# H3 convolution with a bilinear gated unit, forward and backward: forward sums of 2048 elements, a sixth transform by eight residues, early rows in single PSUM banks, filter rows turned whole

## The chip, the cores and the metric

One core of one Trainium2 chip. The metric is the device time of one execution in microseconds: the time before is the median of 3 runs. Engines: PE (TensorE, matrix multiplications and their weight loads), DVE (VectorE), ACT (ScalarE), POOL (GpSimd), SP (SyncE, which issues transfers).

## What is computed

The forward pass, and the gradients of all inputs for a given output gradient, of

```python
xn = layernorm(x)                                  # x = A_q, [2048, 1024]
kv = shift4(k, shift_k) * v                        # causal, four taps, by channel
y  = irfft(rfft(kv padded to 4096) * rfft(ssm_k padded to 4096))[:2048] + kv * ssm_D
g  = silu(((xn @ w_gate) * (xn @ w_up)) @ w_down)  # 1024 -> 3584 -> 1024
out = x + (xn * y) * g
```

for a sequence of 2048 rows and 1024 channels; inputs and outputs are bf16.

## The kernel before

**The matrix part.** The layer norm is made in six chunks of 128-row blocks: blocks (0,1), (1,1), (2,2), (4,4), (8,4), (12,4), written (first, count). DVE takes statistics (L584, L585), ACT a square root (`half_r`, L592), DVE a reciprocal and the normalization (L603). The rows are then turned on PE (as weights, against an identity) into PSUM and copied by ACT to `XNT`: blocks 0 and 1 in halves (L609, L610), 2 to 7 whole (L620, L621), 8 to 15 by `turn_late` (L631 copies, L571 turns). `gu_unit` multiplies them with slabs of `w_gate` and `w_up` (L673, tile `psg`); ACT casts the result (L675, `gut`), DVE forms `h` (tile `hN`, a product of 128x1024; `hN_s` in the first chunks), PE turns it (`turn_pair`, L571, or L724), and it is stored. The last turn of `hN` is made by `flush()`, some steps into the next part, in which h is multiplied with `w_down` (L1032, tile `psbm`, by `bm_first`; 28 steps `fc`, of four matmuls each). The load of the later rows of `w_down` and of `HT` follows the flush on SP. After that comes the backward pass (L1480 to L1642).

**The convolution.** It runs beside the matrix part, slice after slice of 128 channels (`ds` 0 to 7). A generator, `conv_forward`, is advanced by `tick`, which compares the weights that it yields (`F_TOTAL` is their sum, `pe_us` the PE time charged to them) with the progress of the matrix part. Its operations are pinned, so on each engine the order is the order of the program. For each slice there are two forward transforms, of the filter (`hx`) and of `kv`, then a product of spectra and an inverse. A forward transform has a part on PE (`psF`, L234), an eviction by ACT to `SP` (L295) and butterflies on DVE. It takes one of two forms: four residues (`fwd4_half`, 32 matmuls psF of 128x256 per transform) or eight (`fwd8_half` and `fwd8`, 16 matmuls and more of DVE). `EIGHT` lists (slice, kind) in the second form, with kind 0 for `kv` and 1 for the filter; `INV8` lists the slices whose inverse goes by eight. The DVE sums W <- SP are of 128x1024, and `SP` has two buffers, one for each half of the transform.

**The filter rows.** `h_rows(ds)` turns a slice of `ssm_k`: sixteen column blocks of 128, read with a stride of eight elements, each in two halves of 64 rows on two parts of the array (`turn_halves`, L571), into one tile `tr` of the one-buffer pool `ps_tr`; ACT copies it to `hx` (L791).

**PSUM early on.** The early turns take banks of one tile `turns` in `ps_st`, of four banks in a ring (`next_bank`); `keep_busy` writes one of them with dummy matmuls (L534).

What sets the order around the change is the program order for the pinned operations, and for the rest (`issue_after` lines, the layer norm's chunks) a scheduler. The order in which the engines run is fixed when the kernel is built.

Of the kernel before, what the change touches and what calls it, by code (L numbers as in the profile page):

```python
# [19 lines left out]
def build_kernel(  # L20
# [11 lines left out]
    nc = tc.nc  # L32
# [210 lines left out]
    def net(w):  # L243
        w -= 0.95 * pe_us[0]
        pe_us[0] = 0.0
        return w

    def fwd4_half(x, i, wp, psp, first=None):

        pe_us[0] += 1.75  # L250
        SP = wp.tile([P, 2, 2, 512], F32, name="SP", bufs=2)
        for par in range(2):
            ps = psp.tile([P, 2, 2, 256], F32, name="psF")
            cmm(ps[:, 0], T4[par], x, (i, i + 4), first if i == 0 else None, True)
            cmm(ps[:, 1], T4[par], x, (i + 2, i + 6))
            nc.scalar.copy(out=SP[:, :, par], in_=ps[:].rearrange("p s k x -> p s (k x)"))
        return SP

    def fwd4_buf(wp):
        return wp.tile([P, 2, 2, 4, 256], F32, name="W", tag="W")  # L260

    def fwd4_sums(W, SP, i):
        s, q = [SP[:, j].rearrange("p a (k x) -> p (a k) x", k=2) for j in range(2)]
        tt(W[:, 0, i], s, q, ADD)
        tt(W[:, 1, i], s, q, SUB)

# [19 lines left out]

    def fwd8_half(x, i, SP, psp, first=None, held=False):

        pe_us[0] += 0.87
        for j in range(2):  # L290
            r = 2 * i + j
            ps = psp.tile([P, 2, 2, 256], F32, name="psF")
            cmm(ps[:, 0], T4[0], x, (r,), first if r == 0 else None, held)
            cmm(ps[:, 1], T4[0], x, (r + 4,))
            nc.scalar.copy(out=SP[:, :, j], in_=ps[:].rearrange("p s k x -> p s (k x)"))  # L295

    def fwd8(SPs, X, W, C, ahead, late=False):
# [5 lines left out]
        for i in range(2):  # L303
            s, q = [SPs[i][:, j].rearrange("p a (k x) -> p (a k) x", k=2) for j in range(2)]
            tt(W[:, 4 * i:4 * i + 4, :], s, q, ADD)
            tt(W[:, 4 * i + 8:4 * i + 12, :], s, q, SUB)
            yield 2.5
# [213 lines left out]
    ps_gu = pool("ps_gu", 2, space=PSUM)  # L521
    ps_st = pool("ps_st", 1, space=PSUM)
    turns = ps_st.tile([P, 4, 2, 4, P], BF16, name="tr")
    bank = [0]

    def next_bank():
        bank[0] += 1
        return turns[:, bank[0] % 4]

    busy = turns[:, 0].rearrange("p a b x -> p (a b x)").bitcast(F32).rearrange("p (a x) -> p a x", a=4)  # L530

# [45 lines left out]
    def layer_norm(b0, n, x4):  # L577
# [22 lines left out]
        for i in range(n):  # L600
            b = b0 + i
            q, qi = divmod(b, 4)
            last = V.tensor_scalar(x4[:, i, :], x4[:, i, :], mv[:, i, 0:1], RSTD[:, b:b + 1], op0=SUB, op1=MUL)  # L603
            if b < 2:
                for hh in range(2):
                    ps = next_bank()[:, 0]
                    for dc in range(4):
                        d0 = (4 * hh + dc) * P
                        tr_ln[0] = nc.tensor.transpose(ps[:, dc, :], x4[:, i, d0:d0 + P], ident[:])  # L609
                    act_copy[0] = nc.scalar.copy(out=XNT[0][:, 4 * hh:4 * hh + 4, b * P:b * P + P], in_=ps)  # L610
                if b == 0:
                    with tc.issue_after(tr_ln[0].ins):
                        keep_busy(10)
                continue
            if b0 >= 8:
                turn_rows.append((x4[:, i, :], q, qi))
                continue
            ps = next_bank().rearrange("p a b x -> p (a b) x")
            for dc in range(DC):
                tr_ln[0] = nc.tensor.transpose(ps[:, dc, :], x4[:, i, dc * P:(dc + 1) * P], ident[:])  # L620
            act_copy[0] = nc.scalar.copy(out=XNT[q][:, :, qi * P:(qi + 1) * P], in_=ps)  # L621
        c, r0 = divmod(b0, 8)
        return last, root, st(xnn[:, c, r0:r0 + n, :], x4[:, 0:n, :])

    def turn_late():
        ps = turns[:].rearrange("p (h j) i b x -> p h j i (b x)", h=2).rearrange("p h j i (a u) -> p h (j i) a u", u=64)
        for i, (x, q, qi) in enumerate(turn_rows):
            for dc in range(DC):
                tr_ln[0] = turn_halves(lambda hh: ps[:, hh, i, dc], x[:, dc * P:(dc + 1) * P])
        for i, (x, q, qi) in enumerate(turn_rows):  # L630
            act_copy[0] = nc.scalar.copy(out=halves(XNT[q][:, :, qi * P:(qi + 1) * P]), in_=ps[:, :, i])  # L631
        turn_rows.clear()
# [100 lines left out]
    ht_st = [None]  # L733
    EIGHT = ((0, 0), (0, 1), (6, 0), (7, 0), (7, 1))
    INV8 = (2, 4, 5, 6, 7)
# [6 lines left out]
    def conv_forward():  # L742
# [35 lines left out]

        def h_rows(ds):
            if ds == 8:  # L780
                return
            hrow = S_["h", ds]
            hx = S_["hx"] = cf.tile([P, NB, P], BF16, name="hx")
            pe_us[0] += 0.67
            ps = tr_tile()[:].rearrange("p h b x -> p h (b x)").rearrange("p h (b u) -> p h b u", u=64)
            with tc.issue_after(tr_ln[0].ins):
                turn_halves(lambda hh: ps[:, hh, 0], hrow[:, 0, :, 0])
            for b in range(1, 16):
                turn_halves(lambda hh: ps[:, hh, b], hrow[:, b // 8, :, b % 8])
            for c in range(2):  # L790
                nc.scalar.activation(halves(hx[:, 8 * c:8 * c + 8, :]), ps[:, :, 8 * c:8 * c + 8], ACT.Copy, scale=WSC)  # L791
            h_out.append(ds)
            if ds + 1 < 8:
                load_h(ds + 1)

# [30 lines left out]
        def half(ds, x, i, first=None):  # L826
            if (ds, int(first is not None)) not in EIGHT:
                return fwd4_half(x, i, cf, ps_cv, first)
            SP = cf.tile([P, 2, 2, 512], F32, name="SP", bufs=2)
            fwd8_half(x, i, SP, ps_cv, first, True)  # L830
            return SP

        def transform(ds, kind, sp, X, C, ahead, step):
# [10 lines left out]
            W = fwd4_buf(cs)  # L844
            fwd4_sums(W, sp[0], 0)
            step()
# [15 lines left out]
        yield 3.9  # L862
        h_rows(0)
        yield 0.1
        tl = turn_tables(ps_cv)
        sp = [half(0, S_["hx"], i, Dz[:, 0:P]) for i in range(2)]
        for ds in range(8):
# [18 lines left out]
            def behind():  # L886
                calls.append(0)
                if len(calls) % 2 == 0:
                    next(tl, None)
            room = cf.tile([P, 4, 256], F32, name="room", tag="hx")[:] if eight else None  # L890
            yield from transform(ds, int(ds > 0), sph, HX if ds else KX, room, nop1 if eight else lambda c: h_rows(ds + 1) if c == 0 else None,
                                 behind)
            if ds == 0:
                S_["kst"] = st(KFd[0], KX[:])
            if eight:
                h_rows(ds + 1)
            turned(HX, 1, 0, 1)
            yield 1.3
            if ds == 7:
                cf.release()  # L900
                S_["filters"] = False
# [20 lines left out]

    F_TOTAL = 4 * SHIFT_W + 3.0 + 8 * (0.5 + FWD4_W + 1.3 + PROD_W + INV_W) + 10.0 - 0.95 * 8 * (4 * 1.75 + 0.67 + 4 * 0.9)
    F_TOTAL += len(EIGHT) * (FWD8_W - 9.6 + 0.95 * 1.75) - 2.0
# [49 lines left out]
    for p_ in (lnp, lns, tg, bsb):  # L974
        p_.release()
    ps_st.release()
    ps_cv = pool("ps_cv", 2, space=PSUM)
# [70 lines left out]
    pss = [ps_bm.tile([P, D], F32, name="psbm") for i in range(2)]  # L1048
    with tc.issue_after(bm_first(range(4)).ins):
        flush()  # L1050
# [14 lines left out]
    with tc.issue_after(wd_ld.ins):  # L1065
        ht1 = load_ht1()
    fc_ = 4
    while conv_state["filters"]:
# [737 lines left out]
```

## Time and profile before

| | us |
|---|---|
| median of 3 runs (lowest to highest) | 1915.76 (1915.60 to 1915.89) |
| profiled execution, its own time | 1915.97 |
| its span | 1914.2 |
| PE busy (share of span) | 1895.2 (99%) |
| DVE busy | 1550.7 (81%) |
| ACT busy | 637.1 (33%) |
| POOL busy | 334.8 (17%) |
| share of PE in the chain that ended last | 96% |

A line of a timeline reads: start in us, duration of the group, engine, source line and operation, output<-input, array tile and size, count, and in brackets the idle time ahead of it and what released it. A line of the groups reads: busy time of all, mean ns of one, and after the bar the idle time ahead. A line of the waits reads: the engine and what it waited to do, the instruction that released it, the total in us, how many times, the longest. The TensorE clock granted in this execution was 0.999 of full.

### The profile page before, as it was taken

To read this page: it belongs to the slowest core of one execution; us is meant where nothing else is said; L and a number is where in the kernel's file an instruction comes from. 1 tells how busy PE (TensorE), PEld (TensorE's weight loads), DVE (VectorE), ACT (ScalarE), POOL (GpSimd) and SP (SyncE) were. 2 spreads that over 40 slices of the span, in tenths; PEclk is the share of its full clock that TensorE was granted. 3 is DMA by queue.
4 is the path that set the end of the run, shared out by engine and by line. 5 is a ranking of instruction groups with operands and counts; after the bars stand their busy time and mean duration, and the time that the engine had idled before them with its cause. 6 is when DMAs were issued, how large, how long until landed. Compare 5 with 4: busy or idle time off the path is not lost.

```text
span 1914.2 us, 28265 instructions
## 1 busy us (share of the span) xinstructions
PE 1895.2 (99%) x11367; PEld 1014.8 (53%) x11507; DVE 1550.7 (81%) x1711; ACT 637.1 (33%) x927; POOL 334.8 (17%) x465
## 2 busy tenths in 40 slices
PE   8999999999999999999999999999999999999999
PEld 4555555545444456666666665664444444444444
DVE  7999999999988556887999999999995205678862
ACT  5765555546433233432222222222222102011122
POOL 5121212111113220001031221111212101112120
PEclk9999999999999999999999999999999999999999
DMA  8777866769769997677888698585887999889963
GB/s 285 269 251 232 257 224 207 234 233 296 248 228 311 313 306 230 208 239 229 275 264 264 221 266 267 181 286 177 227 245 173 221 203 180 182 176 195 194 162 124
DMA packets 425107, 444.35 MB, mean 232 GB/s; under 512 B 268400, under 2 KB 342796, under 8 KB 410512
## 3 DMA queue, kind: packets, MB, share of 16 engines
q1 hardware_dynamic: 367504, 239.03, 46.7%
q0 software_dynamic: 41152, 174.15, 29.3%
q10 hardware_dynamic: 16320, 29.36, 4.1%
q8 instruction: 90, 1.47, 0.3%
q14 instruction: 41, 0.34, 0.1%
HBM read 193.87 MB, written 189.84 MB: 200 GB/s over the span
## 4 chain that ended last, share of the span: by engine, by line
PE 96%; DVE 1%; issue 1%; ACT 1%; DMA 1%; SPq 0%; ACTq 0%; DVEq 0%
PE psb L1497 20%; PE psx L1642 20%; PE psg L673 19%; PE psb L1480 10%; PE psb L1580 9%; PE psbm L1032 9%; PE psF L234 3%; PE tr L571 1%; PE psI L455 1%; PE psY L1191 1%; PE psY L445 1%; PE psx L1580 1%; DMA U<-in_A_q_dram 1%; ACT U L631 0%; DVE bst L584 0%
## 5 line engine op out<-in xcount | busy, mean ns | idle before, releaser
L673 PE MATMUL psg<-wslab,U 128*128 128x512 bf16 x1728 | 399.0, 380 | 5.2 <-ACT gut L675 1.2
L1497 PE MATMUL psb<-U,U 128*128 128x512 bf16 x1792 | 397.1, 379 | 0.0
L1642 PE MATMUL psx<-U,dgut 128*128 128x512 bf16 x1505 | 331.0, 379 | 1.6
L1642 PEld LDWEIGHTS <-dgut 128*128 128x128 bf16 x1792 | 175.3, 98 | 211.4
L1497 PEld LDWEIGHTS <-U 128*128 128x128 bf16 x1792 | 175.2, 98 | 198.0
L673 PEld LDWEIGHTS <-U 128*128 128x128 bf16 x1792 | 172.4, 98 | 195.0 <-issue 3.5
L1480 PE MATMUL psb<-wdt,U 128*128 128x256 bf16 x1792 | 205.6, 273 | 0.0
L1480 PEld LDWEIGHTS <-U 128*128 128x128 bf16 x1792 | 175.3, 98 | 29.2
L212 DVE TENSOR_TENSOR W<-W 128x1024 f32<-128x1024 f32 (+1 forms) x189 | 186.5, 1003 | 4.1
L1580 PE MATMUL psb<-U,U 128*128 128x512 bf16 x797 | 176.1, 379 | 0.9
L1502 ACT CAST wb<-psb 128x512 bf16<-128x512 f32 x112 | 65.6, 586 | 315.4 <-PE psb L1497 313.4
L1247 DVE SCALAR_TENSOR_TENSOR dkp<-dkT,kT 128x1024 bf16<-128x1024 bf16 (+2 forms) x64 | 78.3, 1224 | 97.7 <-DMA dkT<-DKSHd 96.0
L1032 PE MATMUL psbm<-U,ht 128*128 128x512 bf16 x658 | 145.0, 379 | 0.7
L1580 PEld LDWEIGHTS <-U 128*128 128x128 bf16 x896 | 87.4, 98 | 104.3
L675 ACT CAST gut<-psg 128x512 bf16<-128x512 f32 x156 | 91.6, 589 | 117.0 <-PE psg L673 108.9
L1674 ACT ACTIVATE dx_t<-dxn 128x1024 bf16<-128x1024 f32 x15 | 15.9, 1057 | 323.1 <-DVE dxn L212 317.7
L1032 PEld LDWEIGHTS <-ht 128*128 128x128 bf16 x672 | 65.6, 98 | 78.2
L212 DVE TENSOR_TENSOR U<-U,dht 128x2048 bf16<-128x2048 bf16 x56 | 68.3, 1221 | 46.8 <-ACT dht L1482 46.7
L1482 ACT CAST dht<-psb 128x512 bf16<-128x512 f32 x112 | 65.6, 587 | 116.3 <-PE psb L1480 116.3
L66 POOL DMA_DIRECT2D Hd<-hN x54 | 37.3, 690 | 261.2 <-DVE hN L212 259.0
L1621 ACT CAST wbs<-psb 128x512 bf16<-128x512 f32 x51 | 29.9, 586 | 145.4 <-PE psb L1580 134.4
L212 DVE TENSOR_TENSOR W<-SP 128x1024 f32<-128x1024 f32 x64 | 74.2, 1218 | 1.6 <-ACT SP L295 1.1
(259 smaller groups left out, 2342.2 us busy)
## 6 DMA issues: line engine op xcount, KB each, us to landing
U<-GUd SPq DMA_DIRECT2D x28, 1024.0 KB, 8.9
DGd<-U SPq DMA_DIRECT2D x28, 1024.0 KB, 6.2
GUd<-gut ACTq DMA_DIRECT2D x39, 512.0 KB, 5.8
out_dram<-wb SPq DMA_DIRECT2D x112, 128.0 KB, 4.9
U<-Hd SPq DMA_DIRECT2D x14, 1024.0 KB, 6.7
Hd<-hN POOLq DMA_DIRECT2D x54, 256.0 KB, 5.0
HTd<-hT SPq DMA_DIRECT2D x24, 512.0 KB, 4.1
ht<-HTd SPq DMA_DIRECT2D x18, 512.0 KB, 7.6
```

The costliest lines, as they stand in the source:

```text
L212: pinned(V.tensor_tensor(o, a, b, op))
L234: mm = nc.tensor.matmul(ps[:, k].rearrange("p (c d) -> p c d", c=2), T[:, r, k, :], xr[:, r], start=(n == 0), stop=(n == len(rs) - 1 and ( ...
L673: gu_mm[0] = nc.tensor.matmul(ps[:], XNT[q][:, dc, qi * P:(qi + 1) * P], w[:, dc].rearrange("p a f -> p (a f)"), start=(dc == 0), stop=(dc ...
L675: nc.scalar.copy(out=gut[:, :, i], in_=ps[:].rearrange("p (a f) -> p a f", a=2))
L1032: mm = nc.tensor.matmul(ps[:, dh * 512:(dh + 1) * 512], ht(fc)[:, i * P:(i + 1) * P], WD[fc // 4][:, fc % 4, dh * 512:(dh + 1) * 512], sta ...
L1247: ins = V.scalar_tensor_tensor(prod[:].rearrange("p r d -> p (r d)")[:, lo:H], dkT[:, 0, lo:H], 1.0, kT[:, 0, 13 + m + lo:13 + m + H], op0 ...
L1480: nc.tensor.matmul(ps[:, x * SLW:(x + 1) * SLW], DBMT[2 * hf + g][:, dc, (b % 4) * P:(b % 4 + 1) * P], wdt[:, dc, :], start=(dc == 0), sto ...
L1482: nc.scalar.copy(out=dht[:, 2 * e:2 * e + 2].rearrange("p b f -> p (b f)"), in_=ps[:])
L1497: nc.tensor.matmul(ps[:], XN[b // 4][:, b % 4, dc * P:(dc + 1) * P], dgus[b // 8][:, :, b % 8], start=(b == 0), stop=(b == NB - 1))
L1502: nc.scalar.copy(out=wb[:, dc % 2].rearrange("p a f -> p (a f)"), in_=ps[:])
L1580: nc.tensor.matmul(ps, h[:, f, b, :], DBM[b // 4][:, b % 4, dh * 512:(dh + 1) * 512], start=(b == 0), stop=(b == NB - 1))
L1642: nc.tensor.matmul(ps[:, dh * 512:(dh + 1) * 512], t[n][:, f, i * P:(i + 1) * P], WGU[n][:, f, dh * 512:(dh + 1) * 512], start=(n == 0 and ...
```

## The change

Six things change.

1. The two buffers of `SP`, one for each half, become one tile of both halves, so that the sums W <- SP are operations of 128x2048 elements: two per transform in place of four. The eight-residue form does so where it runs late (`late`).
2. `EIGHT` gets `(5, 0)`: the transform of `kv` of slice 5 goes by eight residues.
3. The early turns get tiles of their own from a pool `ps_st` of four single-bank buffers, in place of banks of one tile; `turn_late` takes its tiles from a second pool of two that replaces the first, and copies two rows at a time.
4. `h_rows` takes an argument `c` and is called twice a slice, for eight column blocks each; each block is turned by one plain 128x128 transpose. Each half has its own tile and its own copy by ACT.
5. The weights change: 0.47 for a call of `h_rows` (0.67 for all before), and `F_TOTAL` with 0.95 (before 0.67).
6. `flush()` comes after `bm_first(range(8))` (before `range(4)`), and `fc_` starts at 8.

```diff
@@ -245,24 +245,30 @@
         pe_us[0] = 0.0
         return w
 
+    sp_tile = [None]
+
+    def sums_of(wp, i):
+        if i == 0:
+            sp_tile[0] = wp.tile([P, 2, 2, 2, 512], F32, name="SP")
+        return sp_tile[0]
+
     def fwd4_half(x, i, wp, psp, first=None):
 
         pe_us[0] += 1.75
-        SP = wp.tile([P, 2, 2, 512], F32, name="SP", bufs=2)
+        SP = sums_of(wp, i)
         for par in range(2):
             ps = psp.tile([P, 2, 2, 256], F32, name="psF")
             cmm(ps[:, 0], T4[par], x, (i, i + 4), first if i == 0 else None, True)
             cmm(ps[:, 1], T4[par], x, (i + 2, i + 6))
-            nc.scalar.copy(out=SP[:, :, par], in_=ps[:].rearrange("p s k x -> p s (k x)"))
+            nc.scalar.copy(out=SP[:, :, i, par], in_=ps[:].rearrange("p s k x -> p s (k x)"))
         return SP
 
     def fwd4_buf(wp):
         return wp.tile([P, 2, 2, 4, 256], F32, name="W", tag="W")
 
-    def fwd4_sums(W, SP, i):
-        s, q = [SP[:, j].rearrange("p a (k x) -> p (a k) x", k=2) for j in range(2)]
-        tt(W[:, 0, i], s, q, ADD)
-        tt(W[:, 1, i], s, q, SUB)
+    def fwd4_sums(W, SP, n):
+        s, q = [SP[:, j].rearrange("p i a x -> p (i a x)") for j in range(2)]
+        tt(W[:, n].rearrange("p i a x -> p (i a x)"), s, q, (ADD, SUB)[n])
 
     def fwd4_outs(X, W, n):
         c, d = W[:, 0], W[:, 1]
@@ -284,7 +290,7 @@
         if PIN[0]:
             tc.keep_in_program_order(ins)
 
-    def fwd8_half(x, i, SP, psp, first=None, held=False):
+    def fwd8_half(x, i, SP, psp, first=None, held=False, whole=False):
 
         pe_us[0] += 0.87
         for j in range(2):
@@ -292,7 +298,7 @@
             ps = psp.tile([P, 2, 2, 256], F32, name="psF")
             cmm(ps[:, 0], T4[0], x, (r,), first if r == 0 else None, held)
             cmm(ps[:, 1], T4[0], x, (r + 4,))
-            nc.scalar.copy(out=SP[:, :, j], in_=ps[:].rearrange("p s k x -> p s (k x)"))
+            nc.scalar.copy(out=SP[:, :, i, j] if whole else SP[:, :, j], in_=ps[:].rearrange("p s k x -> p s (k x)"))
 
     def fwd8(SPs, X, W, C, ahead, late=False):
 
@@ -301,9 +307,13 @@
                 ahead(n - late)
 
         for i in range(2):
-            s, q = [SPs[i][:, j].rearrange("p a (k x) -> p (a k) x", k=2) for j in range(2)]
-            tt(W[:, 4 * i:4 * i + 4, :], s, q, ADD)
-            tt(W[:, 4 * i + 8:4 * i + 12, :], s, q, SUB)
+            if late:
+                s, q = [SPs[1][:, j].rearrange("p i a x -> p (i a x)") for j in range(2)]
+                tt(W[:, 8 * i:8 * i + 8, :].rearrange("p a x -> p (a x)"), s, q, (ADD, SUB)[i])
+            else:
+                s, q = [SPs[i][:, j].rearrange("p a (k x) -> p (a k) x", k=2) for j in range(2)]
+                tt(W[:, 4 * i:4 * i + 4, :], s, q, ADD)
+                tt(W[:, 4 * i + 8:4 * i + 12, :], s, q, SUB)
             yield 2.5
         tt(C[:], W[:, 0:4, :], W[:, 4:8, :], ADD)
         tt(W[:, 0:4, :], W[:, 0:4, :], W[:, 4:8, :], SUB)
@@ -519,15 +529,9 @@
     fg = pool("fg", 2, side="right")
     ps_tr = pool("ps_tr", 1, space=PSUM)
     ps_gu = pool("ps_gu", 2, space=PSUM)
-    ps_st = pool("ps_st", 1, space=PSUM)
-    turns = ps_st.tile([P, 4, 2, 4, P], BF16, name="tr")
-    bank = [0]
-
-    def next_bank():
-        bank[0] += 1
-        return turns[:, bank[0] % 4]
-
-    busy = turns[:, 0].rearrange("p a b x -> p (a b x)").bitcast(F32).rearrange("p (a x) -> p a x", a=4)
+    ps_st = [pool("ps_st", 4, space=PSUM)]
+
+    busy = ps_st[0].tile([P, 4, P], F32, name="tr")
 
     def keep_busy(n):
         for i in range(n):
@@ -603,11 +607,11 @@
             last = V.tensor_scalar(x4[:, i, :], x4[:, i, :], mv[:, i, 0:1], RSTD[:, b:b + 1], op0=SUB, op1=MUL)
             if b < 2:
                 for hh in range(2):
-                    ps = next_bank()[:, 0]
+                    ps = ps_st[0].tile([P, 4, P], BF16, name="tr")
                     for dc in range(4):
                         d0 = (4 * hh + dc) * P
                         tr_ln[0] = nc.tensor.transpose(ps[:, dc, :], x4[:, i, d0:d0 + P], ident[:])
-                    act_copy[0] = nc.scalar.copy(out=XNT[0][:, 4 * hh:4 * hh + 4, b * P:b * P + P], in_=ps)
+                    act_copy[0] = nc.scalar.copy(out=XNT[0][:, 4 * hh:4 * hh + 4, b * P:b * P + P], in_=ps[:])
                 if b == 0:
                     with tc.issue_after(tr_ln[0].ins):
                         keep_busy(10)
@@ -615,20 +619,24 @@
             if b0 >= 8:
                 turn_rows.append((x4[:, i, :], q, qi))
                 continue
-            ps = next_bank().rearrange("p a b x -> p (a b) x")
+            ps = ps_st[0].tile([P, DC, P], BF16, name="tr")
             for dc in range(DC):
                 tr_ln[0] = nc.tensor.transpose(ps[:, dc, :], x4[:, i, dc * P:(dc + 1) * P], ident[:])
-            act_copy[0] = nc.scalar.copy(out=XNT[q][:, :, qi * P:(qi + 1) * P], in_=ps)
+            act_copy[0] = nc.scalar.copy(out=XNT[q][:, :, qi * P:(qi + 1) * P], in_=ps[:])
         c, r0 = divmod(b0, 8)
         return last, root, st(xnn[:, c, r0:r0 + n, :], x4[:, 0:n, :])
 
     def turn_late():
-        ps = turns[:].rearrange("p (h j) i b x -> p h j i (b x)", h=2).rearrange("p h j i (a u) -> p h (j i) a u", u=64)
-        for i, (x, q, qi) in enumerate(turn_rows):
-            for dc in range(DC):
-                tr_ln[0] = turn_halves(lambda hh: ps[:, hh, i, dc], x[:, dc * P:(dc + 1) * P])
-        for i, (x, q, qi) in enumerate(turn_rows):
-            act_copy[0] = nc.scalar.copy(out=halves(XNT[q][:, :, qi * P:(qi + 1) * P]), in_=ps[:, :, i])
+        if turn_rows and len(ps_st) == 1:
+            ps_st[0].release()
+            ps_st.append(pool("ps_s2", 2, space=PSUM))
+        for i in range(0, len(turn_rows), 2):
+            ps = ps_st[1].tile([P, 2, 2, DC, 64], BF16, name="tr2")
+            for j, (x, q, qi) in enumerate(turn_rows[i:i + 2]):
+                for dc in range(DC):
+                    tr_ln[0] = turn_halves(lambda hh: ps[:, hh, j, dc], x[:, dc * P:(dc + 1) * P])
+            for j, (x, q, qi) in enumerate(turn_rows[i:i + 2]):
+                act_copy[0] = nc.scalar.copy(out=halves(XNT[q][:, :, qi * P:(qi + 1) * P]), in_=ps[:, :, j])
         turn_rows.clear()
 
     nop = lambda: None
@@ -731,7 +739,7 @@
     h_out = []
     cv_gone = []
     ht_st = [None]
-    EIGHT = ((0, 0), (0, 1), (6, 0), (7, 0), (7, 1))
+    EIGHT = ((0, 0), (0, 1), (5, 0), (6, 0), (7, 0), (7, 1))
     INV8 = (2, 4, 5, 6, 7)
     SHIFT_W = 8 * 2.3
 
@@ -776,22 +784,23 @@
             st(KSHd[dp], U[6][:].rearrange("p (b d) -> p b d", b=NB))
             yield 2.3
 
-        def h_rows(ds):
+        def h_rows(ds, c):
             if ds == 8:
                 return
             hrow = S_["h", ds]
-            hx = S_["hx"] = cf.tile([P, NB, P], BF16, name="hx")
-            pe_us[0] += 0.67
-            ps = tr_tile()[:].rearrange("p h b x -> p h (b x)").rearrange("p h (b u) -> p h b u", u=64)
+            if c == 0:
+                S_["hx"] = cf.tile([P, NB, P], BF16, name="hx")
+            pe_us[0] += 0.47
+            ps = tr_tile()[:, 0]
             with tc.issue_after(tr_ln[0].ins):
-                turn_halves(lambda hh: ps[:, hh, 0], hrow[:, 0, :, 0])
-            for b in range(1, 16):
-                turn_halves(lambda hh: ps[:, hh, b], hrow[:, b // 8, :, b % 8])
-            for c in range(2):
-                nc.scalar.activation(halves(hx[:, 8 * c:8 * c + 8, :]), ps[:, :, 8 * c:8 * c + 8], ACT.Copy, scale=WSC)
-            h_out.append(ds)
-            if ds + 1 < 8:
-                load_h(ds + 1)
+                nc.tensor.transpose(ps[:, 0, :], hrow[:, c, :, 0], ident[:])
+            for r in range(1, 8):
+                nc.tensor.transpose(ps[:, r, :], hrow[:, c, :, r], ident[:])
+            nc.scalar.activation(S_["hx"][:, 8 * c:8 * c + 8, :], ps, ACT.Copy, scale=WSC)
+            if c == 1:
+                h_out.append(ds)
+                if ds + 1 < 8:
+                    load_h(ds + 1)
 
         def kvs(ds):
             return S_["kvt", ds // 2][:, :, ds % 2 * P:(ds % 2 + 1) * P]
@@ -826,8 +835,8 @@
         def half(ds, x, i, first=None):
             if (ds, int(first is not None)) not in EIGHT:
                 return fwd4_half(x, i, cf, ps_cv, first)
-            SP = cf.tile([P, 2, 2, 512], F32, name="SP", bufs=2)
-            fwd8_half(x, i, SP, ps_cv, first, True)
+            SP = sums_of(cf, i)
+            fwd8_half(x, i, SP, ps_cv, first, True, True)
             return SP
 
         def transform(ds, kind, sp, X, C, ahead, step):
@@ -842,7 +851,7 @@
                     yield net(w)
                 return
             W = fwd4_buf(cs)
-            fwd4_sums(W, sp[0], 0)
+            fwd4_sums(W, sp[1], 0)
             step()
             yield net(2.4)
             fwd4_sums(W, sp[1], 1)
@@ -860,7 +869,8 @@
         yield from shift(0)
         PIN[0] = True
         yield 3.9
-        h_rows(0)
+        h_rows(0, 0)
+        h_rows(0, 1)
         yield 0.1
         tl = turn_tables(ps_cv)
         sp = [half(0, S_["hx"], i, Dz[:, 0:P]) for i in range(2)]
@@ -888,14 +898,16 @@
                 if len(calls) % 2 == 0:
                     next(tl, None)
             room = cf.tile([P, 4, 256], F32, name="room", tag="hx")[:] if eight else None
-            yield from transform(ds, int(ds > 0), sph, HX if ds else KX, room, nop1 if eight else lambda c: h_rows(ds + 1) if c == 0 else None,
+            yield from transform(ds, int(ds > 0), sph, HX if ds else KX, room, nop1 if eight else lambda c: h_rows(ds + 1, c),
                                  behind)
             if ds == 0:
                 S_["kst"] = st(KFd[0], KX[:])
             if eight:
-                h_rows(ds + 1)
+                h_rows(ds + 1, 0)
             turned(HX, 1, 0, 1)
             yield 1.3
+            if eight:
+                h_rows(ds + 1, 1)
             if ds == 7:
                 cf.release()
                 S_["filters"] = False
@@ -920,7 +932,7 @@
         cx.release()
         kst.release()
 
-    F_TOTAL = 4 * SHIFT_W + 3.0 + 8 * (0.5 + FWD4_W + 1.3 + PROD_W + INV_W) + 10.0 - 0.95 * 8 * (4 * 1.75 + 0.67 + 4 * 0.9)
+    F_TOTAL = 4 * SHIFT_W + 3.0 + 8 * (0.5 + FWD4_W + 1.3 + PROD_W + INV_W) + 10.0 - 0.95 * 8 * (4 * 1.75 + 0.95 + 4 * 0.9)
     F_TOTAL += len(EIGHT) * (FWD8_W - 9.6 + 0.95 * 1.75) - 2.0
     F_TOTAL += len(INV8) * (INV8_W - INV_W + 0.95 * 1.8)
     conv = conv_forward()
@@ -973,7 +985,7 @@
     st(RSTN[:], RSd.rearrange("(b p) -> p b", p=P))
     for p_ in (lnp, lns, tg, bsb):
         p_.release()
-    ps_st.release()
+    ps_st[1].release()
     ps_cv = pool("ps_cv", 2, space=PSUM)
     pump, drain, step = make_pump(conv, F_TOTAL)
     cnt = [-5]
@@ -1046,7 +1058,7 @@
     cv_gone.append(True)
     ps_bm = pool("ps_bm", 2, side="right", space=PSUM)
     pss = [ps_bm.tile([P, D], F32, name="psbm") for i in range(2)]
-    with tc.issue_after(bm_first(range(4)).ins):
+    with tc.issue_after(bm_first(range(8)).ins):
         flush()
     for p_ in (ps_gu, fg, fw):
         p_.release()
@@ -1064,7 +1076,7 @@
 
     with tc.issue_after(wd_ld.ins):
         ht1 = load_ht1()
-    fc_ = 4
+    fc_ = 8
     while conv_state["filters"]:
         bm_first([fc_])
         fc_ += 1
```

## The prediction

> **What bounds the kernel now.** I read the page first. PE is busy for nearly the whole span, its first slice excepted, and DVE is full in slices 2 to 8, where the early rows end and the forward convolution begins:
>
> ```profile
> PE 1895.2 (99%) x11367; PEld 1014.8 (53%) x11507; DVE 1550.7 (81%) x1711; ACT 637.1 (33%) x927; POOL 334.8 (17%) x465
> ...
> PE   8999999999999999999999999999999999999999
> ...
> DVE  7999999999988556887999999999995205678862
> ```
>
> So a microsecond of work taken off PE is a microsecond off the end, unless PE is then made to wait. The table by stretches puts 51.6 us of PE in the first 60 and 441.0 in the next 444: PE's waiting lies in the first 60 us (8.4 us, of which 4.7 lie before the first matmul). PE's waits in 0 to 62 us name it:
>
> ```profile
> PE tr L620 <- DVE U L603: 3.2, 1, 3.2
> ...
> PE psg L673 <- ACT gut L675: 1.2, 1, 1.2
> PE tr L609 <- ACT U L610: 0.9, 2, 0.7
> PE psg L673 <- ACT U L675: 0.3, 1, 0.3
> ```
>
> DVE's side of the same stretch, in its timeline:
>
> ```profile
> 20.43 1.04 DVE L212 TENSOR_TENSOR hN_s<-gut_s 128x256 bf16<-128x256 bf16 x1
> ...
> 26.40 1.92 DVE L603 TENSOR_SCALAR U<-U,mv,RSTD 128x1024 bf16<-128x1024 bf16 x4
> ...
> 36.28 0.18 DVE L595 RECIPROCAL rec<-half_r 128x4 f32<-128x4 f32 x1 [1.31 <-ACT half_r L592]
> ```
>
> PE's 3.2 us wait at 27.00 ends when row 26.40 ends its first quarter. From 54.03 (first product of the shift) DVE runs back to back to about 555. Its only idle times there are 1.06 at 74.62 (for SP), 0.97 at 128.42, 0.65 at 240.72 and 0.64 at 248.31 (for gut or U). DVE is hence the second chain, and what counts is where PE takes something from it. That place is the last turn of h:
>
> ```profile
> 509.27 0.68 DVE L212 TENSOR_TENSOR hN<-gut 128x1024 bf16<-128x1024 bf16 x1
> ```
>
> ```profile
> 509.73 1.24 PE L1032 MATMUL psbm<-U,U 128*128 128x512 bf16 x5
> 510.99 0.64 PE L571 MATMUL tr<-ident,hN 64*128 64x64 bf16 x32
> ```
>
> The last product of h ends at 509.95, and PE turns it at 510.99: 1.04 us of slack. Earlier pairs have 4 to 6 (at 417.0, 433 and 468.8: 4.3, 5.2 and 6.0).
>
> **Prices**, from the groups with shapes kept apart:
>
> ```profile
> L234 PE MATMUL psF<-kv,TF 128*128 128x256 bf16 x208 | 25.3, 273 | 0.1
> L571 PE MATMUL tr<-ident,U 64*128 64x64 bf16 x384 | 12.1, 213 | 0.2
> L212 DVE TENSOR_TENSOR W<-SP 128x1024 f32<-128x1024 f32 x64 | 74.2, 1218 | 1.6 <-ACT SP L295 1.1
> L212 DVE TENSOR_TENSOR W<-KX 128x2048 f32<-128x2048 bf16 x16 | 36.6, 2289 | 0.3
> ```
>
> **Slice 5 by eight residues, on PE.** The order of the changed kernel has 16 matmuls psF of 128x256 fewer. Eight of that size (psI at 508.85) start 0.88 us ahead of what follows, 0.11 each: −1.76 us.
>
> **Filter rows turned plainly.** 256 half turns become 128 whole ones. A group of 32 halves stands at 67.40 with the next matmul at 68.50 (1.10), and some 0.15 us goes before it (106.66 to 106.81): 1.25 a slice. Eight plain turns of packed rows (55.55 to 56.00) take 0.45, 0.056 each. Here the loaded rows are spread in memory, one element of every eight; the halves show what that costs, 0.034 each against 0.02 for packed hN. I take 0.06 to 0.065 for a plain one: 16 × 0.064 = 1.02 a slice, so −0.23 × 8 = −1.8. Bounds: 0.056 gives −2.8, and 0.139, the mean of the spread halves' weight loads, gives +7.8 (a rival below). Each slice's rows now go in two groups through the one tr buffer; the copy between (1.0 us of ACT) is covered by the L673 matmuls that the order puts there. Without them it is 1 us at slice 0.
>
> **Sums of 2048 elements, DVE.** By means, two of 1218 less one of 2289 saves 0.147. But neighbours overlap: four of 1024 start 361.95 to 366.50, 1.14 apart, and one of 2048 occupies 2.20 by its starts. So 0.07 each, two a transform, and 15 transforms before the last product of h: −2.0. [...] I take the starts.
>
> **Slice 5's kv by eight residues, DVE.** Eight residues: 506.99 to 523.45 less a product of h (0.6) = 15.9. Four: 361.95 to 371.64 less 0.6 = 9.1. So +6.8 of DVE; with the merged sums +4.8, on a DVE without gaps.
>
> **The wait that merging adds.** The first sum now needs both halves of SP. The evictions end before the sums begin by 0.3 to 10 us everywhere but at slice 0 (copies 72.66 to 76.42, first sum 74.62) and at one later transform, where the first sums cover it. At slice 0 the sums start at about 77.1 (76.42, plus some 0.7 to 0.9 because the filter rows come in two groups): +2.5 on DVE, and all of the convolution and the products of h stand behind it. The three later idle times (0.97 + 0.65 + 0.64 = 2.26) take that back: +0.2 remains.
>
> **Early rows in buffers of their own.** The order shows four things. The second turns of x lose their wait for ACT's copy (0.9 us of the waits). About 1 us more of PE's work lies ahead of the turn that waits 3.2. The product at 20.43 moves into DVE's 2.00 us wait for rows at 18.63, so that U's normalization at 26.40 comes 0.96 earlier. And ACT's half_r at 36.03 no longer queues behind the four copies that hold it, which frees up to 1.31 of DVE. PE, DVE and ACT together come 2.5 us earlier at 55 us: 0.96 + 1.31 + part of the 0.97 wait at 46.47. Bounds: 0 (the k loads, which land near 50.6 beside what the queues hold, hold the shift; it starts at 54.03 now) and 3.5. I take 2.5.
>
> **The flush.** It moves from after 21 psbm matmuls to after 32. Eleven at 0.2155 = 2.37 us of cover, at no cost of its own. The w_down load behind it on SP goes out at 519.41 and takes 6.4 to land; it is needed at about 529. It moves by some 3.5 less the gain ahead, and lands near 527: nothing, with 1 to 2 us in hand. If that cover is gone it costs what the load is late.
>
> **The sum.** Without waits PE would gain 1.76 + 1.8 + 2.5 = 6.1 us. At the flush PE would arrive at 510.99 − 1.76 − 1.8 + 2.37 − 2.5 = 507.3. DVE has its product at 509.95 + 4.8 + 0.2 − 2.5 = 512.45. PE waits 5.2 us in all, some 2 of them already at the pairs turned at 417 to 485, whose slack the same growth eats. So −6.1 + 5.2 = −0.9. The profiled execution's own time is 1915.97, 0.21 above the median of the runs; the difference applies to the median 1915.76: 1914.9.
>
> **Rivals.** *DVE's growth stays covered.* If the late sums at slice 0 don't happen, merging saves 0.147, and products of h come ahead of the sums in DVE's order, PE waits nowhere: 1915.76 − 6.1 = 1909.7. For it: slack of 4 to 6 us nearly everywhere. Against: 1.04 at the flush, and a DVE that is never idle. Chance 0.25.
> *No earlier start.* The k loads hold the shift: PE's gain early is used up, and only −3.6 + 5.2 = +1.6 is left: 1917.4. For it: DVE reaches the shift 3.4 us after the loads have landed, so that a gain of more than that can't be had; against: 2.5 is less. Chance 0.12.
> *The plain turn is slow.* If weights spread in memory load in 0.139 us each and nothing hides that (the mean of the spread halves' loads; packed ones show 0.095), a slice takes 2.22 in place of 1.25: +7.8 on PE, which then arrives at the flush later than DVE. The end: −1.76 + 7.8 − 2.5 = +3.5, 1919.3, slower than before. It decides from about 0.10 a turn, where PE's loss equals its 5.2 us of waiting. For it: spread halves take 1.10 a group, packed ones 0.64. Against: a load runs under the turn before it. [...] Chance 0.13, half of it beyond 0.2%.
> The rest, 0.50, is the forecast: 1912.2 to 1917.5 by the bounds of the early gain and of the sums.
>
> **The numbers.** 0.2% is 3.8 us, about what a measurement of this kernel can tell from no change. Faster by more: the covered case, 0.25. Slower by more: half of the slow turns and a late w_down load or a DVE later than summed on top of no earlier start, 0.14. Within: 0.61. The range takes in the covered case and the slow turns: 1909.5 to 1919.5.
>
> **What would show it.** Right: PE's waits name hN products at the flush and around 417 to 485 with 4 to 6 us in all, and the shift starts near 51.5. The filter groups take about 0.5 each. The first sum at slice 0 shows a wait for SP of 2 to 4. DVE's idle at 128, 240 and 248 is gone. Wrong: PE waits of less than 2 us after 60 us (then the covered case), a shift that starts after 53, or filter groups of 0.8 and more.

## The result, and the profile after

The changed kernel takes 1919.31 us (median), the kernel before 1914.41 in the same comparison: ratio 1.0022 (95% interval 1.0016 to 1.0029), 4.2 us slower by the ratio; the medians are 4.9 apart. The forecast was 0.9 us faster. The spans of the two profiled executions, 1914.2 and 1918.5, differ by 4.3. Executions of one kernel show a mean granted clock of 1.000, or of 0.999 and less with some 2 us more, and their mix moves a median: at 1.000 the changed kernel takes 1917.96 (seven of 15), and the kernel before 1913.5 to 1913.9 in the comparisons below.

The page of the changed kernel first, with the busy times and the row of the merged sums:

```profile
PE 1900.3 (99%) x11363; PEld 1012.6 (53%) x11363; DVE 1554.3 (81%) x1691; ACT 636.6 (33%) x927; POOL 334.3 (17%) x465
...
L212 DVE TENSOR_TENSOR W<-SP 128x2048 f32<-128x2048 f32 x32 | 72.4, 2286 | 3.2 <-ACT SP L301 1.8
```

DVE grew by 3.6 us net, where the sum had 4.8 up to the flush. PE waited nowhere after 60 us in the kernel before, but for 0.2 us. Its waits now, in 60 to 700 us (two more are of 0.2):

```profile
PE psF L234 <- ACT SP L263: 4.0, 4, 1.6
PE psF L234 <- ACT SP L301: 2.0, 2, 1.7
PE tr L796 <- ACT hx L799: 0.6, 1, 0.6
PE tr L796 <- ACT hT L715: 0.3, 1, 0.3
```

Six microseconds wait for the copies to SP; none of them waits for a product of h, which the forecast had named. What ACT itself waits for says why. First the line of the kernel before, then that of the changed one, both in 60 to 520 us:

```profile
ACT SP L256 <- DVE W L212: 1.3, 2, 0.6
```

```profile
ACT SP L263 <- DVE W L212: 13.1, 5, 3.8
```

ACT waits 13.1 us for DVE before it may write SP, and 3.2 more in the form by eight residues. The 1.3 of the kernel before are hardly waits for DVE at all: in both of its gaps, of 0.65 us each, ACT issues a transfer of 0.52 (199.94 to 200.46 in one). The longest wait of PE behind a copy of L263, in the timelines of DVE, ACT and PE around 200 us:

```profile
194.92 4.49 DVE L212 TENSOR_TENSOR W<-SP 128x2048 f32<-128x2048 f32 x2
```

```profile
199.52 1.93 ACT L263 COPY SP<-psF 128x1024 f32<-128x1024 f32 x2 [2.88 <-DVE W L212]
```

```profile
197.06 0.82 PE L234 MATMUL psF<-hx,TF 128*128 128x256 bf16 x6
197.71 1.24 PE L681 MATMUL psg<-wslab,U 128*128 128x512 bf16 x5
200.58 1.95 PE L234 MATMUL psF<-hx,TF 128*128 128x256 bf16 x16 [1.63 <-ACT SP L263]
```

PE has filled both psF buffers for the filter's transform by 197.7. ACT can't empty them: its target, SP, is read by both sums of the kv transform before it, and the second sum ends at 199.4 only. With two buffers, the first half of SP is free after the first two sums of 1024. In the kernel before, DVE and ACT:

```profile
196.85 4.63 DVE L212 TENSOR_TENSOR W<-SP 128x1024 f32<-128x1024 f32 x4
```

```profile
200.55 1.93 ACT L256 COPY SP<-psF 128x1024 f32<-128x1024 f32 x2 [0.65 <-DVE W L212]
```

The next transform's first copy starts 3.70 us after the first of the four sums and ahead of the end of the last, 201.48. In the changed kernel it starts 4.60 after the first sum, 0.11 after both have ended. The same chain stands at 137, 313, 441 and 499 us.

At 499 it costs twice. Behind the waits of 1.67 and 0.32 us the matmuls of 128x512 run at half speed for a while:

```profile
499.11 0.60 PE L234 MATMUL psF<-hx,TF 128*128 128x256 bf16 x4 [1.67 <-ACT SP L301]
500.03 0.60 PE L234 MATMUL psF<-hx,TF 128*128 128x256 bf16 x4 [0.32 <-ACT SP L301]
500.46 5.30 PE L681 MATMUL psg<-wslab,U 128*128 128x512 bf16 x16
```

The table by stretches (PE busy, its count, then the granted clock, the DMA share and GB/s) shows the clock:

```profile
499.00:501.00 2.00, 1.57 (x10) 0.93 0.93 314
501.00:504.00 3.00, 3.00 (x8) 0.50 0.81 303
```

Sixteen matmuls from 500.46 take 5.30 us there, and 3.62 elsewhere (from 192.40, for one): 1.7 us lost. The 1.63 us wait at 200.58 left the clock at 1.00 (199 to 203 us). And in the profile of experiment 7 the same two waits stand at the same place (1.69 and 0.32 us, from 498.40), and the sixteen matmuls behind them take 3.62: the half clock comes in some executions and not in others. No run shows what decides it. The mean clock of 0.999 in eight of the changed kernel's fifteen executions fits such a drop (by an estimate, 1.7 us of the span of 1918.5 are 0.0009); where it fell is seen in the profiled one alone.

Last, the flush. DVE and PE of the changed kernel:

```profile
511.94 0.68 DVE L212 TENSOR_TENSOR hN<-gut 128x1024 bf16<-128x1024 bf16 x1
```

```profile
515.79 1.89 PE L1044 MATMUL psbm<-U,U 128*128 128x512 bf16 x8
517.61 0.64 PE L575 MATMUL tr<-ident,hN 64*128 64x64 bf16 x32
```

The product ends at 512.62, and PE turns it at 517.61, with 5.0 us to spare.

**Where the time came from.** The first pair of h is turned at 114.91 before and at 112.82 after, −2.09. Some 1.7 of that is a half clock which the profiled execution of before has at 27 to 32 us, behind PE's wait of 3.2 us, and the changed one has not; 0.46 is the filter rows' work of two slices. The last is turned at 510.99 and at 517.61, +6.62, of which 2.37 is work moved ahead of it. What follows takes the same time up to that (1403.2 and 1400.9). So +4.25 in all. Between the two turns the work fell by 3.1 at the prediction's prices, so 9.4 us were added: 6.0 of waits for SP, 0.3 for tr and 1.7 of half clock. The list also counts each wait short, from the modelled end of the matmul before it: at 200.58 the five matmuls from 197.71, at 0.2155 each (eight take 1.89, one 0.38), make room for the next at 198.79, so 1.79 us are lost and 1.63 listed. For seven waits that is 1.1. The remaining 0.3 is not explained.

### The profile page after: what moved, and what is told of

It reads as the page before. It is cut to its first block, busy times and chain, and to the rows that moved or that the text cites. A ratio compares the mean times of both kernels' runs of the same rounds, so it can differ in the third digit from the quotient of the medians.

```text
span 1918.5 us, 28097 instructions
## 1 busy us (share of the span) xinstructions
PE 1900.3 (99%) x11363; PEld 1012.6 (53%) x11363; DVE 1554.3 (81%) x1691; ACT 636.6 (33%) x927; POOL 334.3 (17%) x465
## 4 chain that ended last, share of the span: by engine, by line
PE 84%; DVE 11%; issue 2%; ACT 1%; DMA 1%; SPq 0%; DVEq 0%; ACTq 0%
PE psb L1509 20%; PE psx L1654 20%; PE psb L1492 10%; PE psbm L1044 10%; PE psg L681 9%; PE psb L1592 9%; DVE W L212 4%; DVE HX L212 2%; DVE KX L212 2%; PE psF L234 1%; DVE m L212 1%; DVE hN L212 1%; PE psY L1203 1%; PE psY L455 1%; PE psx L1592 1%
## 5 line engine op out<-in xcount | busy, mean ns | idle before, releaser
L681 PE MATMUL psg<-wslab,U 128*128 128x512 bf16 x1792 | 404.8, 380 | 4.2 <-DMA wslab<-in_B_w_gate_dram 2.6
L212 DVE TENSOR_TENSOR W<-SP 128x2048 f32<-128x2048 f32 x32 | 72.4, 2286 | 3.2 <-ACT SP L301 1.8
```

What stands on the lines that cost most here:

```text
L212: pinned(V.tensor_tensor(o, a, b, op))
L681: gu_mm[0] = nc.tensor.matmul(ps[:], XNT[q][:, dc, qi * P:(qi + 1) * P], w[:, dc].rearrange("p a f -> p (a f)"), start=(dc == 0), stop=(dc ...
```

## The experiments

Ratios are against the kernel before; each has its interval, and the microseconds against it are the ratio's distance from 1 times its median. Differences between two experiments are those of their medians.

**1. The sums put back, all else as changed.** `SP = wp.tile([P, 2, 2, 512], F32, name="SP", bufs=2)` again, with four sums of 1024, in both forms. Two of the places:

```diff
-        SP = sums_of(wp, i)
+        SP = wp.tile([P, 2, 2, 512], F32, name="SP", bufs=2)
...
-            fwd4_sums(W, sp[1], 0)
+            fwd4_sums(W, sp[0], 0)
```

> The changed kernel with the forward sums put back: two buffers of SP, one for each half of a transform, and four sums of 1024. All else as changed. Theory S (the single SP tile makes the copies of the next transform wait for both sums, and PE behind them): the waits of psF for SP, 6.0 us after the change, and the stretch at half clock at 501 to 504 us (1.7 us) go; the sums cost DVE 2.0 us more, and PE then waits some 3 us for h products at the flush. About 5 us under the changed kernel, near the kernel before: 1913 to 1914. Theory D (slice 5's longer transform on DVE is what holds PE): the waits stay, and the time is within 1 us of the changed kernel or above it. Theory R (the filter rows in two groups and their copies): as D.

Measured: 1914.81 us, ratio 1.0004 (0.9996 to 1.0012): most of the loss is gone. At a clock of 1.000 it is 1914.80, 3.2 us under the changed kernel and 1.2 over the kernel before (1913.55). PE's waits for SP fell from 6.0 to 2.5 us (ACT's for the sums from 13.1 and 3.2 to 6.2 and 0.5), and eleven of its twelve executions have a mean clock of 1.000. Theory S had them go entirely, and a wait at the flush in their place. That didn't come; PE waits 1.7 us for kv at 295.65 instead. The profiled execution is 7.5 us over the median: it has a wait of 4.6 us for DVE in the backward pass and a mean clock of 0.998, so only its part before 700 us is used.

**2. Without slice 5's eight residues, all else as changed.**

```diff
-    EIGHT = ((0, 0), (0, 1), (5, 0), (6, 0), (7, 0), (7, 1))
+    EIGHT = ((0, 0), (0, 1), (6, 0), (7, 0), (7, 1))
```

> The changed kernel without the transform of kv of slice 5 by eight residues; all else as changed. Theory S: the waits at 137, 200 and 313 us, which lie ahead of slice 5, stay (3.1 us); those at 441 and 499 shrink, since DVE is 6.8 us earlier there, by 1 to 3 us and the half clock with them, while PE has 1.8 us more work: 0 to 3 us under the changed kernel. Theory D: all waits beyond slice 5 go and the time falls to 4 us or more under the changed kernel. Theory R: plus 1.8 us.

Measured: 1914.24, ratio 1.0000 (0.9991 to 1.0008). That is more than theory S allowed: 5.1 us came back (3.7 at a clock of 1.000), where 0 to 3 were expected, and theory D had asked for 4 or more. The waits for SP fell to 1.5 us in all, and ahead of slice 5 too: 0.38 us at 200.8, where the changed kernel has 1.63 at 200.6. By the code, slice 5 can reach back only because `F_TOTAL` counts the entries of `EIGHT`: one entry more changes the pace at which the convolution of all slices is mixed into the matrix part, and with it where PE meets SP and kv. The order shows the change: ahead of the second half of the kv transform at 190.65 the changed kernel has 16 matmuls of psg, this one (192.12) 24. So the two edits cost together: neither alone is to blame for the 4.3 us.

**3. SP in bf16 with two buffers: the wait taken away, the long sums kept.**

```diff
-            sp_tile[0] = wp.tile([P, 2, 2, 2, 512], F32, name="SP")
+            sp_tile[0] = wp.tile([P, 2, 2, 2, 512], BF16, name="SP", bufs=2)
```

> The changed kernel with the SP tile in bf16 and two buffers of it, in the same storage as before, so that a copy of the next transform never waits for the sums of the one before; the sums stay operations of 2048 elements (the spectrum is rounded to bf16 at this point). Theory S: the waits of psF for SP go, 6.0 us and the half clock's 1.7; 5 to 8 us under the changed kernel, 1911 to 1914, and 0 to 2 us under the kernel with halves, which has the longer sums. Theory D: within 1 us of the changed kernel. Theory R: as D.

Measured: 1914.10, ratio 0.9999 (0.9990 to 1.0008). PE's waits in 60 to 700 us:

```profile
PE psF L234 <- DVE kv L212: 1.9, 1, 1.9
PE tr L796 <- ACT hx L799: 1.0, 1, 1.0
PE tr L575 <- DVE hN L212: 0.9, 1, 0.9
```

No wait for SP is left, and ACT no longer waits for the sums. The sums take as long as in f32 (two of them 4.49 us at 306.97, as at 194.92 in the changed kernel), and ACT's waits for them, 13.1 and 3.2 us there, are not in its list: it is the second buffer that did it. SP's storage holds ACT, and the length of the sums does not. But three waits stand in its place, on kv, on hx and, at the flush, on the product of h, and the kernel is no faster than before. In the changed kernel itself PE takes that kv at 297.52, 0.06 us after it ends: there the waits for SP at 137 and 200 us hide the wait for kv.

**4. The long sums alone, on the kernel before.** The first edit of the change and nothing else.

> The kernel before with only the forward sums changed: one SP tile and two sums of 2048 elements a transform. Theory S: PE waits for SP's copies as in the changed kernel at 137, 200 and 313 us (3.1 us) and less after slice 5; the late first sum of slice 0 adds nothing to PE: 2 to 6 us over the kernel before. Theory D: no wait on PE, DVE 2.0 us less: 0 to 1 us under the kernel before. Theory R: as D.

Measured: 1917.69, ratio 1.0018 (1.0010 to 1.0027), 3.4 us slower. At a clock of 1.000 it is the same (1916.97 against 1913.55). PE waits 2.2 us for SP, four times, and ACT 9.5 for the sums. The waits of PE lie at 202, 253, 315 and 367 us, two of them not where they were expected. Theory D and theory R, which gave a gain, fall as the whole cause; the 1.2 us beyond the listed waits are explained only in part, by their being counted short.

**5. Slice 5 alone, on the kernel before.** `(5, 0)` in `EIGHT`, nothing else.

> The kernel before with slice 5's kv by eight residues alone. By the prediction's sum: PE 1.76 us less, DVE 6.8 more, of which idle DVE takes some 1 to 2 back; the product before the flush comes 4.5 to 5.5 us later and PE waits there for 4 to 5 us: 2 to 3.5 us over the kernel before. If the slack takes the growth: 1.8 under it.

Measured: 1921.56, ratio 1.0041 (1.0027 to 1.0055), 7.8 us slower. The last turn of h, in PE's timeline:

```profile
506.61 0.41 PE L571 MATMUL tr<-ident,hN 64*128 64x64 bf16 x16
512.49 0.61 PE L571 MATMUL tr<-ident,hN 64*128 64x64 bf16 x16 [5.48 <-DVE hN L212]
```

```profile
510.00:513.00 3.00, 0.51 (x16) 0.88 1.02 418
513.00:516.00 3.00, 3.00 (x12) 0.55 0.36 130
```

The wait that the prediction put at the flush is there, 5.5 us, and a stretch at a clock of 0.55 behind it, which costs some 1.3. The cover is not that of the kernel before: there 21 matmuls of psbm and eight of psI stand ahead of the turn, here 16 of psbm alone (503.06 to 506.61). The expected 2 to 3.5 had neither. By the profiles the difference is 4.7, and 6.4 without the half clock early on, which this one hasn't by an estimate (its mean clock is 0.999, and the drop at the flush makes 0.9991 by itself): 5.5 and 1.3 at the flush and 0.9 for kv and SP, less 1.8 of PE's work, make 5.9. The median is 0.85 above the profiled execution.

**6. Slice 5 and the later flush.** The kernel before with `(5, 0)`, `bm_first(range(8))` and `fc_ = 8`.

> The kernel before with slice 5's kv by eight residues and the flush after 32 matmuls of psbm in place of 21. If the wait for the last product of h at the flush (5.5 us with slice 5 alone) is what made slice 5 cost, 11 matmuls of cover take 2.4 us of it, and the stretch at half clock behind it (1.3 us) goes with a shorter wait: 2.4 to 4 us under the kernel with slice 5 alone. If slice 5's cost lies elsewhere: no change.

Measured: 1915.47, ratio 1.0006 (0.9997 to 1.0015), some 6 us under experiment 5. The wait at the flush is 1.2 us and the clock behind it isn't halved (31 matmuls of psbm from 514.90 take 7.08). That is more than the 4 us expected, because the turn moved by more than 11 matmuls: from behind 16 of psbm to behind 32 and eight of psI, 4.3 us of cover, which is what the wait lost. The later flush therefore is what makes slice 5 bearable.

**7. The flush put back, all else as changed.** `bm_first(range(4))`, `fc_ = 4`.

> The changed kernel with the flush back after 21 matmuls. After the change the last product of h ends 5 us ahead of its turn, since PE has already lost more to SP's copies than DVE to slice 5. So the flush is worth nothing there: within 0.5 us of the changed kernel. If it has cover to give: 2.4 us over it.

Measured: 1919.02, ratio 1.0023 (1.0014 to 1.0032): by the medians the same as the changed kernel, as expected. But all ten executions have a clock of 1.000, and those of the changed kernel at 1.000 take 1917.96: like with like, the later flush is worth some 1 us there. The earlier one stands behind 16 matmuls of psbm again, and PE waits 0.7 us at it.

**8. The early rows alone, on the kernel before.** The pool `ps_st` of four buffers and the second pool in `turn_late`.

> The kernel before with only the early rows in buffers of their own. By the prediction 2.5 us less. If the load of the gate slab takes the place of the waits removed (1.7 us of PE's wait at 15 us after the change): 0.5 to 1.5 less. If the gain in the trace was only the half clock at 28 us of one execution: none.

Measured: 1911.78, ratio 0.9986 (0.9978 to 0.9995), 2.7 us faster. 1.7 of it shows at a clock of 1.000 (1911.78 against 1913.51); for the rest, all eleven executions have 1.000, and of before only 17 of 27. PE's wait for row 26.40 of the timeline (3.2 us) is 1.0, that for ACT's copies is gone, but the load of the slab of w_gate now holds PE 2.6 us where it held it 0.3.

**9. The filter rows alone, on the kernel before.** The new `h_rows` with its calls and weights.

> The kernel before with only the filter rows turned plainly, in two groups a slice. By the prediction: 1.8 us less PE, so 1.8 us less, if no group waits for the one tr buffer. By the copies seen after the change (0.6 at 107 us and 0.3 at 319 us of waits for ACT): 0.9 us less. Theory R (turns of spread rows slow): no gain or a loss.

Measured: 1915.40, ratio 1.0005 (0.9997 to 1.0014). The turns are cheap: in the changed kernel eight of them stand 0.49 us apart from what follows (63.79 to 64.28). But PE waits 0.6 us for kv at 301.5 us, and the gate slab 0.7 more than before. No gain can be measured, where 0.9 to 1.8 were expected; at a clock of 1.000 (three executions) it is 0.1 slower.

**10. Early rows, filter rows and later flush: without the long sums and slice 5.**

> The changed kernel with the sums in halves again and without slice 5's eight residues: the early rows, the filter rows and the later flush are left of the change. If SP's storage and slice 5 are the two things that cost, nothing waits: the rows save 1.8 us of PE, the early rows up to 2 (their gain was in part the half clock at 28 us that the profile of the kernel before happened to have): 2 to 4 us under the kernel before, 1910.5 to 1912.5. If the filter rows or the early turns cost something by themselves, it is 1914 or more.

Measured: 1911.90, ratio 0.9988 (0.9979 to 0.9997). It is as fast as the early rows alone, within what was expected, and both beat the two kernels. PE waits 0.6 us for kv.

**11. What costs taken out, slice 5 kept.** SP in bf16 with two buffers, filter rows in halves, flush after 14 steps.

> The changed kernel with the filter rows turned in halves as before, SP in bf16 with two buffers (the spectrum is rounded to bf16 at this point), and the flush after 14 steps. What the runs showed to cost is out, slice 5's shorter PE work and the early rows stay. Without waits it is 1.8 us under the kernel with the early rows alone, near 1910; if DVE's product kv before slice 4 and others hold PE as they did (0.7 to 1.9 us), slice 5 gives nothing: 1911.5 to 1913.

Measured: 1913.16, ratio 0.9993 (0.9984 to 1.0002). PE waits 1.5 us for kv and 0.7 us for the load of w_down: the first takes most of the 1.8 us that slice 5 saves, and the second is the wait that a later flush risks. That is the second of the expected cases (1911.5 to 1913), and just above it.

## Why the prediction was wrong, point by point

**The step that failed is "the wait that merging adds".** It looked at who reads SP, and found the first sum late at slice 0 only. It did not look at who writes it next. One tile for both halves is free when both sums are done; two tiles are free one after the other. ACT's copies of the next transform wait for that, the two psF buffers stay full, and PE stands. This was put at nothing, and measured 6.0 us of PE's waits and 1.7 of half clock in the changed kernel. Experiments 3 and 4 show it from both sides: the sums alone cost 3.4 us, and with storage that doesn't wait most of the loss is gone. Not all of the 6.0 is the merging, though: 2.5 are left with two buffers (experiment 1). The part that had been seen was sized well: the first sum at slice 0 starts at 74.01, where 77.1 less the early gain, 74.6, was expected; its wait is 1.8 us, just under the 2 to 4 named as a sign.

**The bound on DVE was right, the kernel's use of it was not.** The last product of h was forecast to end at 512.45, and ended at 512.62. Some of that is luck: the first sum of slice 0 came 0.6 us earlier than forecast, and the way from there to the product took 0.8 longer. PE was to come at 507.3 and wait 5.2, but came at 517.6. With slice 5 alone (experiment 5) the wait is 5.5 us and lies where the prediction put it, but behind 16 matmuls and not 32, so that the two numbers are near each other by chance; with 32 it is 0.9 to 1.2 (experiments 3 and 6). It can take a half clock with it (0.55 over 3 us in experiment 5), which the prediction had no term for.

**Slack was surveyed for h alone.** PE also consumes kv. In the kernel before the product kv ends at 301.46 and PE takes it at 302.93: 1.5 us. What PE gains on DVE ahead of that beyond the 1.5 is lost there; it shows as 0.3 us in experiment 2, 0.6 to 0.7 in 5, 6, 9 and 10, and 1.5 to 1.9 in 1, 3 and 11.

**The early start was mis-sized.** The shift starts at 52.65, 1.38 earlier, not 2.5: DVE waits 2.1 us for PE's matmuls to free the buffer it writes. PE's gain alone is 2.7 us (1.0 to 4.2) in experiment 8, near the 2.5, but by another way: 1.7 at a like clock, and for the rest the half clock, which the prediction did not see in its own trace (0.73 granted at 27 to 29 us, 0.50 at 29 to 31, 0.92 at 31 to 33). A smaller misreading there bears on no sum: of PE's 8.4 us of waiting 1.43 lie before the first matmul, not 4.7.

**The filter rows were priced right and gained nothing.** 0.06 a turn, as taken; the rival with 0.139 falls. The spread weights do load longer, 147 ns each against 98 for packed ones (60 to 520 us of the changed kernel), as that rival had it, but the load is hidden: eight spread turns take 0.49 us, where eight such loads make 1.18, and eight packed ones 0.45. What PE saves goes in part into the wait for kv.

**The sums were priced right.** Two of 2048 take 4.49 us, four of 1024 took 4.63: 0.07 for each merge, the price by starts. The low end of the prediction's range, 1912.2, is 2.7 us under its forecast, with some 0.16 for each of the 30 merges. No run shows that price: the means before give 0.147, and the starts, before and after, 0.07.

**The later flush** was costed at nothing in the sum; beside slice 5 alone it is worth some 6 us, in the changed kernel some 1 us at a like clock, because PE is late for other reasons.

What stays open is how the loss of 4.3 divides between the sums and slice 5: each taken out alone brings nearly all of it back (experiments 1 and 2). How much of slice 5's part is the pace, through `F_TOTAL`, and how much DVE's longer transform is open too: no run held the one and changed the other. The prediction had costed the pace at nothing.

## What to carry to other kernels

When two buffers become one, list the next writer of each half with the last reader before it, not only the next reader: the first buffer's early release is what the second one's writer lived on. Survey the slack of everything that the bound engine takes from another (here kv, hx and SP beside h) before a saving on it is counted. Merging operations saves only what their starts show, 0.07 us each here, which a single wait of PE outweighs. And a half clock of 1.7 us that comes in some executions can stand for a gain or hide one: it did so for the early rows and for the later flush.

## What the runs showed of the hardware

Waits of PE were followed by some 3 us at half clock in some places and not in others. In the kernel before, the wait of 3.2 us that ends at 27.00 has a clock of 0.50 at 28 to 31 us behind it; in experiment 5 the 5.5 at the flush has 0.55 at 513 to 516; in the changed kernel the 2.0 in all at 497 to 500 us has 0.50 at 501 to 504. The profiled executions of experiments 6 and 9, with waits of 3.2 and 2.9 us for the same row as before, have a mean clock of 0.999, and that of experiment 1, with the 4.6 in the backward pass, 0.998; where it fell in them is not shown. After 1.63 us at 200.58 the changed kernel's clock stayed at 1.00. The profiled executions of experiments 4 and 8, with waits of 1.6 and 1.0 us for that row, and of experiment 7, with the same 2.0 as the changed kernel, have a mean of 1.000. So a stall cost 1.3 to 1.7 us beyond itself where the stretch behind it was seen, and the same stall did so in one execution and not in another.
